# Chunks of 128 tokens computed as two halves of 64 with a state between them, in a fused attention and feed-forward kernel

## The chip, the cores and the metric

The kernel runs on one core of a Trainium2 chip, as one launch. The metric is the time of the device for the whole kernel in microseconds (us), the median of its runs. Five engines work beside each other, each in its own order: TensorE (PE: matmuls into PSUM), VectorE (DVE), ScalarE (ACT), GpSimd (POOL) and SyncE (SP, which starts transfers). They wait for one another through semaphores. All arithmetic is in f32.

## What is computed

Two blocks follow each other. The first is an attention block with a decaying state for each of 4 sequences and 8 heads of 48, over 768 tokens. The second is a feed-forward block over the 3072 rows of 384 that come out.

```python
# batch, n_heads, seq, head_dim = (4, 8, 768, 48)
for t in range(S):
    kt, vt, rt = (k[:, :, t], v[:, :, t], r[:, :, t])
    cur = np.einsum('bhd,bhe->bhde', u[None] * kt, vt)
    y[:, :, t] = np.einsum('bhd,bhde->bhe', rt, state + cur)
    state = w[None, :, :, None] * state + np.einsum('bhd,bhe->bhde', kt, vt)
# x: (3072, 384) from y;  d_ff = 1024
h = x @ w_in
h_max = np.max(h, axis=-1, keepdims=True)
e = np.exp(h - h_max)
sm = e / (np.sum(e, axis=-1, keepdims=True) + 1e-09)
solu = h * sm
mu = np.mean(solu, axis=-1, keepdims=True)
var = np.mean((solu - mu) ** 2, axis=-1, keepdims=True)
ln = (solu - mu) / np.sqrt(var + 1e-06) * g_ln
out = ln @ w_out
```

The recurrence over tokens is computed in chunks. Within a chunk, the tokens meet through a matrix of scores (r and k, each weighed by powers of w, of which only the part with earlier keys counts; the diagonal, with u, is computed apart). What lies before the chunk comes in through the state.

## The kernel before, where the change touches it

There are 24 chunks, called units: 6 chunks in each of 4 sequences, in the order chunk by chunk, sequence by sequence. Unit i is the attention of one chunk; its feed-forward input stage (`ffn_in`, the tensor `h_ps`) comes two units later and its output stage (`ffn_out`, `o_ps`) five further on. The instructions stand in the order in which they are written here; nothing is moved by a scheduler. The file also holds a general path, taken only if the data leave certain ranges; with these inputs it does not run, and no part of what follows is about it.

For one unit, `turn_r` and `turn_k` transpose r and k on TensorE (the first nine units; later ones are transposed by transfers, through the buffers `halves`), `diagonal` writes the own term of every token into AT, `scores` computes keys times queries, `take_scores` copies the part with earlier keys into AT, `heads` adds state times r and v times AT to y, `take_y` copies y out of PSUM, `outer` makes k times v, and `update` moves the state on.

```python
    T, P = 128, 64               # tokens of a chunk, rows of a head (48 used)
    # ... cut ...
    psA = ctx.enter_context(tc.tile_pool(name="psA", bufs=1, space=PSUM))
    psH = ctx.enter_context(tc.tile_pool(name="psH", bufs=1, space=PSUM))
    psM = ctx.enter_context(tc.tile_pool(name="psM", bufs=2, space=PSUM))
    # ... cut ...
    units = [(b, c) for c in range(C) for b in range(B)]
    # ... cut ...
    pss = [psA.tile([128, HP, T], F32, name=f"at{n}") for n in range(4)]
    for ps in pss[:2]:
        nc.vector.memset(ps, 0.0)
    # ... cut ...
    def diagonal(i):
        X = live[i]
        AT = X["AT"] = apool.tile([128, H, T], F32, name="AT", bufs=3)
        for h in range(H):
            nc.scalar.activation(out=AT[:, h, :], in_=ident, func=ACT.Copy, scale=X["own"][:, h])

    def turn_r(i):
        rT = factors(i)["rT"]
        ps = pss[2]
        for a in range(HP):
            nc.tensor.transpose(ps[:, a, :], pair(rpads[i % NLD], a), ident)
        nc.vector.tensor_mul(rT, ps, fore)

    def turn_k(i):
        X = live[i]
        ps = pss[3]

        for a in range(HP):
            nc.tensor.transpose(ps[:, a, :], pair(X["kp"] if i > 0 else kpads[0], a), ident)
        if i > 0:
            nc.scalar.copy(out=X["kT"], in_=ps)
        else:
            nc.vector.tensor_mul(X["kT"], ps, back)

    def scores(i):
        X = live[i]
        ps = pss[2:] if i > LA + LO and i % 2 else pss[:2]
        for a in range(HP):
            for c in range(2):
                for q in range(2):
                    rows = slice(q * P, q * P + D)
                    nc.tensor.matmul(ps[q][ts(c, P), a, c * P :], X["kT"][rows, a, ts(c, P)],
                                     X["rT"][rows, a, c * P :], start=True, stop=True)
        X["scores"] = ps

    def take_scores(i):
        A4 = live[i]["AT"].rearrange("p (a q) t -> p a q t", q=2)
        for q in range(2):
            nc.vector.copy_predicated(A4[:, :, q, :], later.to_broadcast([128, HP, T]),
                                      live[i]["scores"][q])

    def parts(m):

        a, n = divmod(m, 3)
        at = {0: [(0, 0)], 1: [(0, 32), (1, 64)], 2: [(1, 96)]}[n]
        return [(2 * a + q, a * 2 * (D + 32) + off) for q, off in at]

    inner = [[(m,) + p for m in range(g, 12, 4) for p in parts(m)] for g in range(4)]
    inner = [group[n] for n in range(4) for group in inner]

    def heads(i):
        b, c = units[i]
        X = live[i]
        vt, AT, St = vts[i % NV], X["AT"], states[b]
        vf = vt.rearrange("p h d -> p (h d)")
        y_ps = psM.tile([128, KD, 128], F32, tag="m", name="y_ps")
        last = {m: n for n, (m, h, at) in enumerate(inner)}
        opened = set()

        def into(m, lhsT, rhs, stop):
            j, g = divmod(m, 4)
            nc.tensor.matmul(y_ps[32 * g : 32 * g + 32, j, :], lhsT, rhs, start=(g not in opened),
                             stop=stop, skip_group_check=True)
            opened.add(g)

        if c > 0:
            for m in range(12):
                a, n = divmod(m, 3)
                into(m, St[:, a].rearrange("p q d -> p (q d)")[:, ts(n, 32)], X["rT"][:, a, :],
                     False)
        for n, (m, h, at) in enumerate(inner):
            into(m, vf[:, at : at + 32], AT[:, h, :], last[m] == n)
        X["y"] = y_ps

    def take_y(i):
        X = live[i]
        X["xT"] = fpool.tile([128, KD, 128], F32, name="xT", bufs=LA + 1)
        nc.scalar.copy(out=X["xT"], in_=X["y"])

    def outer(chunks):

        chunks = [i for i in chunks if i < N and units[i][1] < C - 1]
        if not chunks:
            return
        kv_ps = psM.tile([128, 2, HP, D], F32, tag="m", name="kv_ps")
        for n, i in enumerate(chunks):
            X, vt = live[i], vts[i % NV]
            X["kv"] = kv_ps[:, n]
            for a in range(HP):
                for g in range(4):
                    h = 2 * a + g // 2
                    nc.tensor.matmul(X["kv"][ts(g, 32), a], X["kp"][:, h, ts(g % 2, 32)],
                                     vt[:, h, 0:D], start=True, stop=True)

    def update(i):
        b, c = units[i]
        if c == C - 1:
            return
        kv_ps, St = live[i]["kv"], states[b]
        for q in range(2):
            wT = pw[ts(q, P), 0, 7].unsqueeze(2).to_broadcast([P, HP, D])
            S = St[ts(q, P), :, q]
            if c > 0:
                nc.vector.tensor_add(S, kv_ps[ts(q, P)], S)
                nc.gpsimd.tensor_mul(S, S, wT)
            else:
                nc.vector.tensor_mul(S, kv_ps[ts(q, P)], wT)
```

The loop over units has an opening, in which one unit is done per turn beside the conversion of the weights (`convert_a` is a ScalarE pass, `low`), and a steady part with two units per turn. The opening, cut to the order of the steps that matter here:

```python
    for i in range(-2, LA + LO):                  # LA, LO = 2, 5
        j = i - LA
        # ... cut: loads ...
        if i >= LA:
            ffn_in(j)
        # ... cut ...
        for p in now:
            convert_a(p)
            # ... cut ...
        if -2 < i:
            turn_r(i + 2)
            if i >= LA:
                unit(j)
            if i < 0 or i >= LA:
                sum_own(i + 2)
            turn_k(i + 2)
        # ... cut ...
        if 0 <= i + 1:
            scores(i + 1)
            take_scores(i + 1)
        # ... cut ...
        if 0 <= i:
            heads(i)
            take_y(i)
            outer([i])
            update(i)
        # ... cut ...
        if 0 <= i:
            diagonal(i + 2)
        # ... cut ...
```

The steady part, with what the change moves:

```python
    for i in range(LA + LO, N + LA + LO, 2):
        # ... cut: loads, decay_k, decay_r, weigh, deviation, halve_ln, diagonal, join_ln, join_rk ...
        if j < N and not late:
            ffn_in(j)
            unit(j)
        # ... cut ...
        ffn_out(l)
        # ... cut ...
        if j + 1 < N:
            ffn_in(j + 1)
        # ... cut ...
        if j + 1 < N:
            unit(j + 1)
        if i == N - 1:
            heads(i)
            take_y(i)
        ffn_out(l + 1)
        # ... cut ...
        now = [n for n in (i + 1, i + 2) if n < N]
        for n in now:
            scores(n)
        for n in now:
            take_scores(n)
        now = [n for n in (i, i + 1) if n < N]
        for n in now if i < N - 1 else []:
            heads(n)
            take_y(n)
        if late:
            halve_rk(i + 4)
        outer(now)
        for n in now:
            update(n)
        # ... cut ...
```

`unit` reads h: ScalarE's exp, VectorE's product with h, then two passes of ScalarE.

## Time and profile before

| what | value |
|---|---|
| time, median of 3 runs | 353.0 us (352.12 to 353.31) |
| span of the profiled execution | 350.7 us |
| granted TensorE clock, mean | 0.998 |
| instructions in the trace | 8480 |
| data moved by transfers | 52.76 MB, mean 150 GB/s |

A profile's page gives, for each engine, how long it was busy and its share of the span; then the span in 40 slices, where each digit is the busy share of a slice in tenths (9 is 90% or more); then the chain of work that ended last, followed back from the last instruction, as shares by engine and by line. Further views list groups of instructions (line, engine, operation, tiles, shapes, count, then busy us and mean ns of one, then idle time of the engine before them and what ended it) and instructions in order of time (start, duration, engine, line, operation, and in brackets idle time before it). "PEld" is TensorE's loading of weights, which overlaps with its matmuls. `128*32 128x64` means 128 rows of contraction, 32 columns of weights, and 64 columns that stream through. Matmuls are pipelined, so their durations overlap; starts say more than durations. The lines on which the reading rests are shown in the prediction.

### The profile page before, as it was taken

Reading aid. Unit: us, or ns where it says so; the run is one execution under the profiler, and the core shown is the slowest. Engines: PE = TensorE matmul, PEld = TensorE weight load, DVE = VectorE, ACT = ScalarE, POOL = GpSimd, SP = SyncE. Lnnn points to the kernel's source line nnn. Section 1 sums busy time; section 2 is a strip of 40 time slices with the busy share of each in tenths; the row PEclk is TensorE's granted clock in tenths of the full one; section 3 lists DMA queues with packets and bytes.
Section 4 is the critical chain, followed back from the end, with each engine's and each line's share of the span. In section 5 each row is a group of like instructions: output and inputs, shape, how many; then the busy total and the mean of one; then the engine's idle time right before and its main releaser. Section 6 shows DMA issues by size and latency. Waiting matters only on the chain.

```text
span 350.7 us, 8480 instructions
## 1 busy us (share of the span) xinstructions
PE 334.1 (95%) x3427; PEld 204.6 (58%) x3427; DVE 210.7 (60%) x347; ACT 240.3 (69%) x457; POOL 179.0 (51%) x196
## 2 busy tenths in 40 slices
PE   2699999999999999999999999999999999999993
PEld 2485566655664665575575575575575475555563
DVE  7795888896477568378368368469466162323420
ACT  3765988988858966866866866866867755546510
POOL 3889667789259449539539529629624000000000
PEclk9999999999999999999999999999999999999999
DMA  7999996269999999887999989855993723554541
GB/s 168 265 241 237 234 209 94 46 104 196 186 179 163 225 188 134 195 151 130 182 157 147 202 146 136 202 127 109 144 172 62 129 68 64 125 127 101 135 104 33
DMA packets 164877, 52.76 MB, mean 150 GB/s; under 512 B 157916, under 2 KB 161244, under 8 KB 164828
## 3 DMA queue, kind: packets, MB, share of 16 engines
q1 hardware_dynamic: 164684, 51.92, 79.6%
q8 instruction: 29, 0.48, 0.6%
q10 hardware_dynamic: 144, 0.20, 0.2%
q14 instruction: 20, 0.16, 0.2%
HBM read 26.94 MB, written 4.72 MB: 90 GB/s over the span
## 4 chain that ended last, share of the span: by engine, by line
PE 81%; ACT 7%; DMA 3%; issue 2%; DVE 2%; POOL 2%; SPq 0%; ACTq 0%; POOLq 0%; DVEq 0%
PE o_ps L896 34%; PE h_ps L814 30%; PE y_ps L761 9%; PE at L728 5%; ACT AT L693 3%; ACT halves L864 2%; DVE solu L826 1%; DMA halves<-halves 1%; PE kv_ps L791 1%; ACT e L817 1%; DMA g_sb<-in_moe_g_ln_dram 1%; POOL kp L669 1%; DMA wq<-in_w_dram 1%; ACT solu L828 1%; ACT e L829 1%
## 5 line engine op out<-in xcount | busy, mean ns | idle before, releaser
L814 PE MATMUL h_ps<-w_in_sb,xT 128*128 128x512 f32 x288 | 129.0, 597 | 1.6 <-DVE ma L534 0.8
L896 PE MATMUL o_ps<-w_out_sb,lnT 128*128 128x384 f32 (+1 forms) x400 | 127.5, 474 | 0.1
L896 PEld LDWEIGHTS o_ps<-w_out_sb,lnT 128*128 128x128 f32 x400 | 74.9, 190 | 53.1 <-issue 8.1
L814 PEld LDWEIGHTS h_ps<-w_in_sb,xT 128*128 128x128 f32 x288 | 53.5, 190 | 63.2 <-issue 57.4
L804 POOL TENSOR_TENSOR state<-state,pw 64x192 f32<-64x192 f32 x32 | 27.6, 861 | 68.8 <-DVE state L803 67.2
L693 ACT ACTIVATE AT<-ident,own 128x128 f32<-128x128 f32 x192 | 58.6, 390 | 5.0 <-DVE own L687 5.0
L864 ACT COPY halves<-solu 128x2048 uint16<-128x2048 uint16 x24 | 45.4, 1892 | 3.1 <-DMA halves<-halves 3.1
L669 POOL TENSOR_TENSOR kp<-kpad,kdec 128x512 f32<-128x512 f32 x24 | 41.6, 1735 | 6.9 <-ACT kdec L623 6.3
L828 ACT ACTIVATE solu<-solu,st 128x1024 f32<-128x1024 f32 x24 | 27.5, 1146 | 24.3 <-DVE solu L826 24.3
L817 ACT ACTIVATE e<-h_ps 128x1024 f32<-128x1024 f32 x24 | 24.4, 1019 | 25.3 <-PE h_ps L814 25.2
L735 DVE COPY_PREDICATED AT<-later,at 128x512 f32<-128x512 uint32 x48 | 31.7, 731 | 15.2 <-PE at L728 15.2
L858 DVE COPY lnT<-halves 128x2048 uint16<-128x2048 uint16 x24 | 33.6, 1420 | 6.9 <-DMA halves<-halves 6.6
L824 DVE RECIPROCAL st<-sums 128x1 f32<-128x1 f32 x24 | 3.9, 163 | 54.4 <-ACT e L817 54.1
L835 POOL TENSOR_SCALAR st<-st 128x1 f32<-128x1 f32 x24 | 7.3, 304 | 49.3 <-ACT e L829 49.2
L826 DVE SCALAR_TENSOR_TENSOR solu<-h_ps,st,e 128x1024 f32<-128x1024 f32 x24 | 30.8, 1284 | 2.1
L858 DVE COPY rk<-halves 128x2048 uint16<-128x2048 uint16 x15 | 29.3, 1956 | 0.0
L777 ACT COPY xT<-y_ps 128x384 f32<-128x384 f32 x24 | 11.5, 478 | 22.4 <-PE y_ps L761 22.4
L683 POOL TENSOR_TENSOR rku<-rku,rpad 128x384 f32<-128x384 f32 x23 | 25.6, 1114 | 1.8
L761 PE MATMUL y_ps<-AT,vt 128*32 128x128 f32 x768 | 26.3, 279 | 0.0
L898 ACT ACTIVATE o<-o_ps,st 128x384 f32<-128x384 f32 (+1 forms) x25 | 13.8, 554 | 18.0 <-PE o_ps L896 11.3
L728 PE MATMUL at<-rk 48*64 48x128 f32 (+1 forms) x768 | 26.2, 266 | 0.0
L829 ACT ACTIVATE e<-solu 128x1024 f32<-128x1024 f32 x24 | 25.4, 1057 | 0.8
(83 smaller groups left out, 345.5 us busy)
## 6 DMA issues: line engine op xcount, KB each, us to landing
raw<-in_moe_w_in_dram SPq DMA_DIRECT2D x12, 512.0 KB, 5.4
raw<-in_moe_w_out_dram SPq DMA_DIRECT2D x16, 384.0 KB, 4.3
kpad<-in_k_dram SPq DMA_DIRECT2D x24, 192.0 KB, 5.1
rpad<-in_r_dram SPq DMA_DIRECT2D x24, 192.0 KB, 5.4
vt<-in_v_dram SPq DMA_DIRECT2D x24, 192.0 KB, 5.0
out_dram<-o SPq DMA_DIRECT2D x23, 192.0 KB, 3.4
halves<-halves SPq DMA_TRANSPOSE x39, 4.9
u_bc<-in_u_dram ACTq DMA_DIRECT2D x1, 192.0 KB, 3.6
```

Source lines behind the costliest of these rows:

```text
L669: nc.gpsimd.tensor_mul(X["kp"].rearrange("p h d -> p (h d)"), kpads[i % NLD].rearrange("p h d -> p (h d)"), kdec.rearrange("p a d -> p (a ...
L693: nc.scalar.activation(out=AT[:, h, :], in_=ident, func=ACT.Copy, scale=X["own"][:, h])
L728: nc.tensor.matmul(ps[q][ts(c, P), a, c * P :], X["kT"][rows, a, ts(c, P)], X["rT"][rows, a, c * P :], start=True, stop=True)
L735: nc.vector.copy_predicated(A4[:, :, q, :], later.to_broadcast([128, HP, T]), live[i]["scores"][q])
L761: nc.tensor.matmul(y_ps[32 * g : 32 * g + 32, j, :], lhsT, rhs, start=(g not in opened), stop=stop, skip_group_check=True)
L814: nc.tensor.matmul(h_ps[:, ts(n, NX)], X["xT"][:, j, :], w_in_sb[:, j, ts(n, NX)], start=(j == 0), stop=(j == KD - 1))
L826: nc.vector.scalar_tensor_tensor(out=solu, in0=X["h"], scalar=rs, in1=X["e"], op0=ALU.mult, op1=ALU.mult, accum_out=tot)
L828: nc.scalar.activation(out=solu, in_=solu, func=ACT.Identity, scale=-float(dff), bias=tot)
L829: nc.scalar.activation(out=X["e"], in_=solu, func=ACT.Square, accum_out=ss)
L858: nc.vector.tensor_copy(out=words.bitcast(U16).rearrange("p n (t o) -> p o n t", o=2), in_=turned)
L864: nc.scalar.copy(out=both.rearrange("p (o n) -> p o n", o=2), in_=split(X["solu"]))
L896: nc.tensor.matmul(o_ps, X["lnT"][:, f, :], w_out_sb[:, f, part], start=(f == 0), stop=(f == KF - 1))
```

## The change

Every chunk of 128 tokens is still one unit, but its attention is computed as two halves of 64 tokens. Scores are only formed between tokens of the same half, so a block of 64 x 64 for each half replaces the 128 x 128 block of which only one triangle counts. What the second half needs of the first comes through a middle state, which is the state before the chunk plus k times v of the first half. The products of v and scores then have 64 tokens on each side: those of the first half lie in the upper 64 rows of TensorE's array, those of the second half in the lower 64 rows, and both can be in the array at once. k times v is split into the two halves in the same way, because the middle state needs the first alone.

PSUM is dealt out anew. Scores take two banks instead of four, with two units side by side in each. y of one half lies in one bank, y of the other in another. In the opening, the transposes of r and k use the two rotating buffers of `psM` that y uses too. In the steady part, y of the first unit of a pair lies in the two banks of `h_ps`.

The diff, cut to its core:

```diff
-    pss = [psA.tile([128, HP, T], F32, name=f"at{n}") for n in range(4)]
-    for ps in pss[:2]:
-        nc.vector.memset(ps, 0.0)
+    pss = [psA.tile([128, 2, HP, U], F32, name=f"at{q}") for q in range(2)]      # U = 64
...
     def diagonal(i):
-        AT = X["AT"] = apool.tile([128, H, T], F32, name="AT", bufs=3)
+        AT = X["AT"] = apool.tile([128, H, U], F32, name="AT", bufs=3)
         for h in range(H):
-            nc.scalar.activation(out=AT[:, h, :], in_=ident, func=ACT.Copy, scale=X["own"][:, h])
+            nc.scalar.activation(out=AT[:, h, :], in_=same, func=ACT.Copy, scale=X["own"][:, h])
...
     def turn_r(i):
-        ps = pss[2]
+        ps = psM.tile([128, HP, T], F32, tag="m", name="tr_ps")
...
     def turn_k(i):
-        ps = pss[3]
+        ps = psM.tile([128, HP, T], F32, tag="m", name="tk_ps")
...
     def scores(i):
         for a in range(HP):
             for c in range(2):
                 for q in range(2):
-                    nc.tensor.matmul(ps[q][ts(c, P), a, c * P :], X["kT"][rows, a, ts(c, P)],
-                                     X["rT"][rows, a, c * P :], start=True, stop=True)
+                    nc.tensor.matmul(pss[q][ts(c, U), i % 2, a, :], X["kT"][rows, a, ts(c, U)],
+                                     X["rT"][rows, a, ts(c, U)], start=True, stop=True)
...
-    def heads(i):
+    def within(i, shared=False):
+        if shared:
+            both = psH.tile([128, dff], F32, tag="h", name="y_ps")
+            y = [both[:, c * NX : c * NX + KD * U] for c in range(2)]
+        else:
+            y = [psM.tile([128, KD * U], F32, tag="m", name="y_ps") for _ in range(2)]
...
+        for n, (m, h, at) in enumerate(inner):
+            j, g = divmod(m, 4)
+            for c in range(2):
+                nc.tensor.matmul(X["y"][c][ts(g, 32), j, :], vf[ts(c, U), at : at + 32],
+                                 AT[ts(c, U), h, :], start=(g not in opened), stop=closes,
+                                 skip_group_check=True)
...
+    def carried(i):
+        for c, St in enumerate((states[units[i][0]], X["mid"])):
+            if c == 0 and units[i][1] == 0:
+                continue
+            for m in range(12):
+                nc.tensor.matmul(X["y"][c][ts(g, 32), j, :],
+                                 St[:, a].rearrange("p q d -> p (q d)")[:, ts(n, 32)],
+                                 X["rT"][:, a, ts(c, U)], start=False, stop=True, ...)
...
     def take_y(i):
-        nc.scalar.copy(out=X["xT"], in_=X["y"])
+        for c in range(2):
+            nc.scalar.copy(out=X["xT"][:, :, ts(c, U)], in_=X["y"][c])
...
     def outer(chunks):
-                    nc.tensor.matmul(X["kv"][ts(g, 32), a], X["kp"][:, h, ts(g % 2, 32)],
-                                     vt[:, h, 0:D], start=True, stop=True)
+                    for c, dst in enumerate(X["kv"]):
+                        nc.tensor.matmul(dst[ts(g, 32), a], X["kp"][ts(c, U), h, ts(g % 2, 32)],
+                                         vt[ts(c, U), h, 0:D], start=True, stop=True)
+
+    def middle(i):
+        for q in range(2):
+            to, kv = X["mid"][ts(q, P), :, q], X["kv"][0][ts(q, P)]
+            if c > 0:
+                nc.vector.tensor_add(to, kv, St[ts(q, P), :, q])
+            else:
+                nc.scalar.copy(out=to, in_=kv)
 
     def update(i):
-            if c > 0:
-                nc.vector.tensor_add(S, kv_ps[ts(q, P)], S)
-                nc.gpsimd.tensor_mul(S, S, wT)
-            else:
-                nc.vector.tensor_mul(S, kv_ps[ts(q, P)], wT)
+            nc.vector.tensor_add(S, X["kv"][1][ts(q, P)], X["mid"][ts(q, P), :, q])
+            nc.gpsimd.tensor_mul(S, S, wT)
...  the opening: outer(i) and middle(i) right after ffn_in(j); turn_k before unit(j)
         if i >= LA:
             ffn_in(j)
+            outer([i])
+            middle(i)
...
             turn_r(i + 2)
+            turn_k(i + 2)
             if i >= LA:
                 unit(j)
-            if i < 0 or i >= LA:
                 sum_own(i + 2)
-            turn_k(i + 2)
...  the steady part
-        now = [n for n in (i + 1, i + 2) if n < N]
+        now = [n for n in (i, i + 1) if n < N - 1] if i < N - 1 else []
+        for n in (i + 1, i + 2):
+            if n < N:
+                scores(n)
+        if now:
+            outer(now)
+        if i + 1 < N:
+            take_scores(i + 1)
         for n in now:
-            scores(n)
+            middle(n)
+        if i + 2 < N:
+            take_scores(i + 2)
         for n in now:
-            take_scores(n)
-        now = [n for n in (i, i + 1) if n < N]
-        for n in now if i < N - 1 else []:
-            heads(n)
+            within(n, n == i)
+        for n in now:
+            carried(n)
             take_y(n)
-        outer(now)
         for n in now:
             update(n)
```

## The prediction

> **What bounds the kernel now.** I read the page first: the busy shares, the forty slices, and the chain that ended last by engine and by line.

> ```profile
> PE 334.1 (95%) x3427; PEld 204.6 (58%) x3427; DVE 210.7 (60%) x347; ACT 240.3 (69%) x457; POOL 179.0 (51%) x196
> PE   2699999999999999999999999999999999999993
> PE 81%; ACT 7%; DMA 3%; issue 2%; DVE 2%; POOL 2%; SPq 0%; ACTq 0%; POOLq 0%; DVEq 0%
> ```

> TensorE is 95% busy and carries 81% of the chain; only the first slices are not full. A busy TensorE need not be a full one, so the second view is TensorE's instructions in order of time, for one pair of chunks in the steady loop.

> ```profile
> 148.06 1.96 PE L728 MATMUL at<-rk 48*64 48x128 f32 x64
> 149.95 0.86 PE L761 MATMUL y_ps<-rk,state 128*32 128x128 f32 x24
> 150.63 1.06 PE L761 MATMUL y_ps<-AT,vt 128*32 128x128 f32 x32
> 151.50 0.84 PE L761 MATMUL y_ps<-rk,state 128*32 128x128 f32 x24
> 152.16 1.06 PE L761 MATMUL y_ps<-AT,vt 128*32 128x128 f32 x32
> 153.03 0.86 PE L791 MATMUL kv_ps<-vt,kp 128*32 128x48 f32 x64
> 153.83 5.42 PE L814 MATMUL h_ps<-w_in_sb,xT 128*128 128x512 f32 x12
> ```

> Read start to start: scores of two chunks 1.89 us, the four y groups 3.08, kv 0.80: the attention stage of a pair takes 5.77 us, the feed-forward stages after it about 20.8, and the pattern returns every 26.6 us. Every f32 matmul leaves two records. The third view is the groups with shapes kept apart.

> ```profile
> L728 PE MATMUL at<-rk 48*64 48x128 f32 x384 | 26.2, 286 | 0.0
> L728 PE MATMUL at<-rk 48*64 48x64 f32 x384 | 21.2, 245 | 0.0
> L761 PE MATMUL y_ps<-AT,vt 128*32 128x128 f32 x768 | 26.3, 279 | 0.0
> L761 PE MATMUL y_ps<-rk,state 128*32 128x128 f32 x480 | 17.1, 275 | 0.0
> L791 PE MATMUL kv_ps<-vt,kp 128*32 128x48 f32 x640 | 9.8, 206 | 0.2 <-issue 0.2
> ```

> A mean of 206 to 286 ns against far shorter starts means records overlap on different tiles of the array. In the single records of the trace one tile takes its next record after 109 ns with 128 columns, 42.5 ns with 48, and about 58 ns with 64 (the scores' second half, where it has work). Records for other tiles start 6.7 ns apart. So two things set a group: columns per tile, and 6.7 ns per record.

> The scores show the waste that the change is after: the upper 64 rows of keys stream 128 columns, 16 records at 109 ns for a pair, 1.74 us of the 1.89, while the tiles of the 64-column half stand idle part of the time.

> [...] 64 kv records take 0.80 us, and their mean pitch is 10.6 ns. [...] the pair loses about 0.29 us over pure streaming at three changes, so about 0.1 us each. [...]

> **The change, part by part, for a steady pair.** Before, pure streaming: scores 16 x 0.109 = 1.74; y per chunk 6 + 8 steps of four tiles at 0.109, for two chunks 3.06; kv 16 x 0.0425 = 0.68; sum 5.48, plus 0.29 for the changes of mode = 5.77.
> - Scores: all blocks 64 x 64, 16 steps of 0.058 = 0.93 (−0.81).
> - V times scores: 32 matmuls per chunk, on eight tiles (two row halves, four column groups), 64 columns. A tile needs 56 ns (scaled between the 42.5 and the 109), eight records need 8 x 6.7 = 53, so 7 ns a record: 128 records 0.91 instead of 1.75 (−0.84).
> - State times r: twice as many, half as wide, still four tiles: 24 steps of 56 ns = 1.34 instead of 1.31. Nothing saved.
> - kv: 128 records on eight tiles, now bound by records: 128 x 6.7 = 0.86 instead of 0.68 (+0.18).
> - One more change of mode (64x64, 64x32, 128x32): +0.1.

> After: 0.93 + 0.86 + 0.91 + 1.34 + 0.39 = 4.43 us. I add 0.1 for a new wait: the first chunk's y now lies in the banks of h, so the next h matmul waits for two ScalarE copies of 192 columns (about 0.22 each from 0.38 for 384, plus some 0.35 of signals), and the second chunk's 0.68 us of state products hides all but this. So 4.53, a saving of 1.25 us per pair.

> Beside TensorE: the predicated copies halve (0.65 to about 0.39 us, four per pair), VectorE gains four adds of 0.38 us for the middle state; that is about +0.5 us on an engine with 17.0 of 26.6 busy. ScalarE's eight diagonal writes fall from 0.306 to about 0.25 each, 0.9 us less per pair. In the attention stage the middle state should be there at 2.8 us, TensorE wants it at 3.05: close, but no wait.

> **The first 80 us are another matter.** Here turning r and k by TensorE used two banks of its own; now it shares the two rotating buffers with y. The second half of y therefore waits until ScalarE has copied kT out. In the changed program that copy stands behind exp and the weight conversion; before it came later still, but y did not wait for it. ScalarE's instructions of the kernel before, in order of time:

> ```profile
> 59.71 1.02 ACT L817 ACTIVATE e<-h_ps 128x1024 f32<-128x1024 f32 x1 [1.05 <-PE h_ps L814]
> ...
> 60.72 1.01 ACT L519 ACTIVATE low<-raw 128x384 uint32<-128x384 uint32 x2
> ...
> 64.62 0.57 ACT L715 COPY rk<-at 128x512 f32<-128x512 f32 x1
> ```

> From the end of h: about 1.1 for exp, 0.93 for the conversion, 0.47 for kT, 0.5 more where the middle state is a ScalarE copy (first chunk of each sequence): kT is out after 2.55 or 3.05 us. TensorE would reach y after 1.93 (0.97 transposes, 0.43 kv, 0.53 scores). With 0.45 and 0.34 to 0.67 of products to follow, the gap between two h stages is 3.8 to 3.95 us, against 3.2 to 3.9 now. So from 36 to 78 us the change brings nothing, or loses a little. The start may come 0.2 us sooner (VectorE and ScalarE do less before it).

> After that, at 98 to 110 us, ScalarE is late behind a transposing transfer; the chain in order of time:

> ```profile
> 98.50 5.07 DMA halves<-halves
> ...
> 103.64 1.90 ACT halves L864
> 105.55 2.35 ACT AT L693 x8
> 107.89 1.01 ACT e L817 x2
> ...
> 110.54 5.42 PE h_ps L814 x12
> ```

> TensorE alone would get there 1.6 us sooner; ScalarE, with three times eight lighter diagonal writes on this way (3 x 0.43), about 1.3 to 1.4. I take 1.4 us at 110.54.

> **Sum.** 1.4 + five pairs x 1.25 = 6.25 + pair 19/20 1.1 (kv half needed where there was none, before 5.43) + pair 21/22 0.75 (before 5.09, now 0.68 of kv that was not there) + last chunk 0.1 = 9.6 us. 353.0 − 9.6 = 343.4 us.

> **Rivals.** (a) Records cost more than 6.7 ns in the new mode, or upper and lower rows do not run at once: for it, no 64x32 tiles in the profile before; against it, the scores' 64x64 tiles. Then V times scores stays at 1.75 and kv goes to 1.36, the pair saves about 0, and the kernel lands near 353, or above it. (b) Waits on ScalarE and VectorE eat the gain, as y, its copies and the middle state are now links in one chain inside a stage shorter by a fifth: for it, the 0.25 us of slack above; against it, ScalarE idle 1.6 us before each xT copy. A wait of 0.5 us per pair makes 347. (c) Transfers become the bound: the share of the 16 DMA engines is 0.87 to 1.04 in the steady stretches. Against it: the stretch at 94 to 121 us ran at 1.13 with TensorE busy 26.72 of 27.0, and the transposes of the loop land several us before their use. Then 350. (d) The first 80 us do better, as pairs of matmuls shrink there too and ScalarE has less to do: 341.

> **Range and chances.** The pair's saving is 1.25 ± 0.4 over eight pairs, ± 3 us, the opening ± 2; together about ± 4, a little longer towards slow: 339 to 349. Faster by over 2% means under 345.9: 0.74; slower by over 2%: 0.03.

> **What would show it.** In the changed profile, a pair's attention stage of about 4.5 us; scores of a pair under 1.1 us; V times scores at about 7 ns a record; kv longer than now by 0.2 us; TensorE waits for ScalarE's kT copy inside y in the first 80 us and no wait for the middle state in the loop; h stages up to 78 us at the times of before. I am wrong if a record of the new groups costs over 10 ns, or if waits of TensorE on ScalarE or VectorE sum to over 5 us after 110 us.

## The result and the profile after

The change makes the kernel slower: 417.56 us (416.61 to 419.48) against 352.92 us for the kernel before on the same chip, a ratio of 1.184 (95% interval 1.180 to 1.189). The prediction was 343.4 us with a range of 339 to 349. One run of the experiments below, 415.11 us of the kernel with one burst, was in the slower state that some executions show.

The page of the changed kernel, its engines, TensorE's busy tenths and granted clock in 40 slices, the queue that the page calls instruction, and the chain that ended last:

```profile
PE 351.5 (85%) x5539; PEld 210.8 (51%) x5539; DVE 212.3 (51%) x385; ACT 236.5 (57%) x491; POOL 181.3 (44%) x206
PE   2778999999599779869949959969978979789994
PEclk9999899999989989989989999998999999969998
q8 instruction: 45, 0.74, 0.7%
PE 11%; ACT 0%; issue 0%
```

TensorE was 95% busy and is now 85% busy. Its slices dip to 4 to 7 in a regular pattern, and so does its clock (0.998 on average before, 0.959 now). The other engines' shares are smaller than before (ScalarE 57% instead of 69%, VectorE 51% instead of 60%, GpSimd 44% instead of 51%), so none of them has become the bound. The chain of the changed kernel breaks off after 11% of the span and is of no use here. The row that turned out to matter is an inconspicuous one, the instruction queue: 45 packets of 16 KB. In the kernel before it reads:

```profile
q8 instruction: 29, 0.48, 0.6%
```

The attention stage of one pair in the steady part, TensorE in order of time (start, duration, line, tile shape, columns, count, idle time before it):

```profile
138.76 1.16 PE L734 MATMUL at<-rk 48*64 48x64 f32 x64
139.85 1.38 PE L807 MATMUL kv_ps<-vt,kp 64*32 64x48 f32 x125
...
143.43 1.46 PE L772 MATMUL y_ps<-AT,vt 64*32 64x64 f32 x122 [2.08 <-issue]
144.81 0.31 PE L785 MATMUL y_ps<-rk,state 128*32 128x64 f32 x5
147.54 0.47 PE L785 MATMUL y_ps<-rk,state 128*32 128x64 f32 x18 [2.42 <-issue]
...
149.47 1.22 PE L839 MATMUL h_ps<-w_in_sb,xT 128*128 128x512 f32 x1
```

The stage took 10.71 us (138.76 to 149.47) where it had taken 5.77. Two gaps of over 2 us lie in it, one a few records into V times scores and one inside a run of like matmuls (state times r). "Issue" says that nothing the profile knows released them: no engine, no transfer of data. The groups with shapes kept apart, at the end of each line idle time and its releaser:

```profile
L772 PE MATMUL y_ps<-AT,vt 64*32 64x64 f32 x1536 | 24.2, 229 | 25.5 <-issue 23.7 <-ACT rk L723 1.6
L807 PE MATMUL kv_ps<-vt,kp 64*32 64x48 f32 x1408 | 17.7, 217 | 3.9 <-issue 3.8
L785 PE MATMUL y_ps<-rk,mid 128*32 128x64 f32 x576 | 16.7, 249 | 8.4 <-issue 8.4
L734 PE MATMUL at<-rk 48*64 48x64 f32 x768 | 16.0, 232 | 0.0
L785 PE MATMUL y_ps<-rk,state 128*32 128x64 f32 x480 | 14.0, 251 | 5.1 <-issue 5.1
```

These issue waits sum to 41 us; in the kernel before they were 0.2 us.

**Where the gaps lie.** Take TensorE's records in order, weight loads, matmuls and its own semaphore and control instructions counted one each, as all are instructions. In the changed kernel all 20 gaps of over 0.7 us that are put down to issue, and one that the view puts down to ScalarE (0.81 us at 117.94), come before a record whose number leaves 193 when divided by 256. The other waits of over 0.7 us, for transfers and engines, do not. The packets of the instruction queue, 16 KB each, follow TensorE's count: 11160 instructions make 44 blocks of 256 and 45 packets are listed, the kernel before has 6927, which make 28 blocks, and 29 packets are listed. So the gaps lie where a new block of 256 begins, by these counts one packet to a block. Single entries of the trace show the order of events; here for the two gaps of the pair above:

```
block entered   last record   next block's first record   packet of the instruction queue
139.88          141.14        143.43                      starts 141.11, takes 0.88
143.43          144.90        147.54                      starts 145.15, takes 0.93
```

From entering one block to executing the first instruction of the next takes 3.5 and 4.1 us, though the 256 instructions were used up after 1.3 and 1.5 us. Over all 21 gaps it is 2.6 to 5.6 us, 4.1 in the mean. The kernel before has one trace of this that I passed over: its single issue wait (0.2 us in the groups shown before, at 126.86 us) also lies at a record with remainder 193. It was already at the edge.

**The clock.** The trace's record of the granted clock lists nine stretches at half speed, seven of 3.413 us and one of twice that within the span, and one at its end. The kernel before has none before its end. In a stage that such a stretch falls into, large matmuls take longer:

```profile
182.41 7.11 PE L839 MATMUL h_ps<-w_in_sb,xT 128*128 128x512 f32 x12
```

The same stage takes 5.42 us at full clock, 1.69 less, about half of the stretch's 3.41. The stretch from 148.43 us follows the two gaps of 2.08 and 2.42 us above, with 1.7 us of matmuls between them. What sets a stretch off is in no view.

### The profile page after: what moved, and what is told of

Its sections match the earlier page's. It is cut to its first block, busy times and chain, and to the rows that moved or that the text cites. A ratio compares the mean times of both kernels' runs of the same rounds, so it can differ in the third digit from the quotient of the medians.

```text
span 414.9 us, 12795 instructions
## 1 busy us (share of the span) xinstructions
PE 351.5 (85%) x5539; PEld 210.8 (51%) x5539; DVE 212.3 (51%) x385; ACT 236.5 (57%) x491; POOL 181.3 (44%) x206
## 5 line engine op out<-in xcount | busy, mean ns | idle before, releaser
L839 PE MATMUL h_ps<-w_in_sb,xT 128*128 128x512 f32 x288 | 135.3, 621 | 0.8 <-ACT xT L794 0.8
L794 ACT COPY xT<-y_ps 128x192 f32<-128x192 f32 x48 | 13.3, 320 | 71.9 <-PE y_ps L785 69.6
L701 ACT ACTIVATE AT<-same,own 128x64 f32<-128x64 f32 x192 | 48.4, 337 | 3.5 <-DVE own L695 3.5
L772 PE MATMUL y_ps<-AT,vt 64*32 64x64 f32 x1536 | 24.2, 229 | 25.5 <-issue 23.7
L677 POOL TENSOR_TENSOR kp<-kpad,kdec 128x512 f32<-128x512 f32 x24 | 35.7, 1491 | 6.4 <-ACT kdec L628 5.8
L883 DVE COPY rk<-halves 128x2048 uint16<-128x2048 uint16 x15 | 32.7, 2178 | 0.0
L772 PEld LDWEIGHTS y_ps<-AT,vt 64*32 64x32 f32 x1536 | 18.9, 107 | 26.4 <-issue 23.4
L690 POOL TENSOR_TENSOR rku<-kpad,u_bc 128x384 f32<-128x384 f32 x23 | 29.8, 1297 | 0.0
L684 POOL TENSOR_TENSOR rp<-rpad,rdec 128x512 f32<-128x512 f32 x15 | 28.2, 1879 | 0.0
L830 DVE TENSOR_TENSOR state<-kv_ps,mid 64x192 f32<-64x192 f32 x40 | 14.1, 354 | 27.2 <-PE y_ps L785 26.6
```

Source lines behind the costliest of these rows:

```text
L677: nc.gpsimd.tensor_mul(X["kp"].rearrange("p h d -> p (h d)"), kpads[i % NLD].rearrange("p h d -> p (h d)"), kdec.rearrange("p a d -> p (a ...
L684: nc.gpsimd.tensor_mul(X["rp"].rearrange("p h d -> p (h d)"), rpads[i % NLD].rearrange("p h d -> p (h d)"), rdec.rearrange("p a d -> p (a ...
L690: engine.tensor_mul(rku, kpads[i % NLD][:, :, 0:D], u_bc)
L701: nc.scalar.activation(out=AT[:, h, :], in_=same, func=ACT.Copy, scale=X["own"][:, h])
L772: nc.tensor.matmul(X["y"][c][ts(g, 32), j, :], vf[ts(c, U), at : at + 32], AT[ts(c, U), h, :], start=(g not in opened), stop=closes, skip_ ...
L839: nc.tensor.matmul(h_ps[:, ts(n, NX)], X["xT"][:, j, :], w_in_sb[:, j, ts(n, NX)], start=(j == 0), stop=(j == KD - 1))
```

## The experiments

**Theory.** TensorE runs out of instructions. Each matmul of the program leaves two records, each with a weight load (the 32 matmuls of a pair's scores leave 64 records; the page lists 5539 matmul records and 5539 weight loads): four instructions. The pair's attention stage had 240 records, 480 instructions, in 5.8 us; now it has 416 records, 832 instructions, in one burst of tiny matmuls. **Rival.** The new tiles (64 rows by 32 columns, upper and lower rows) or the middle state stall by themselves in a way that the profile doesn't show. My texts for the runs count instructions where they say records: the "830 TensorE records" of the first are the 832 instructions, and the "384" and "128 more records" of two later ones are 192 and 64 records.

### The same matmuls, standing apart

The opening is that of the kernel before (units 0 to 6 in chunks of 128). In the steady part the scheme of the change is kept, but its pieces stand between the feed-forward stages:

```diff
     ffn_in(j)
+    outer_two(mine)                  # k times v of both chunks
     ffn_out(l)
+    within(i, "y"); carried(i)       # V times scores, state times r
     ffn_in(j + 1)
+    scores(i + 1); scores(i + 2)
     ffn_out(l + 1)
-    scores, outer, within, carried of both chunks in one burst
+    within(i + 1, "y"); carried(i + 1)
```

> Opening as in the kernel before; from then on the split scheme of the change with the same matmuls and tile shapes, but its pieces stand apart, each between two feed-forward stages (at most some 300 TensorE records between two stages of large matmuls, where the change has some 830 in a row). Theory (TensorE runs out of instructions: they arrive in blocks of 256, some 4 us each, and the changed attention stage asks for more than three blocks at once): the 1 to 4 us gaps that no engine explains go away, and so do the stretches at half clock; 350 to 356 us. Rival (the tiles of 64 x 32 in upper and lower rows stall by themselves, or wait for the middle state): the gaps stay with the pieces; 395 us or more.

Measured: 356.63 us (356.57 to 357.21), ratio to the kernel before 1.010 (1.008 to 1.013), clock 0.997. TensorE in order of time:

```profile
153.51 0.86 PE L855 MATMUL at<-AT,vt 64*32 64x64 f32 x64
154.29 0.54 PE L865 MATMUL at<-rk,state 128*32 128x64 f32 x24
154.65 0.52 PE L865 MATMUL at<-rk,mid 128*32 128x64 f32 x24
155.10 5.42 PE L921 MATMUL h_ps<-w_in_sb,xT 128*128 128x512 f32 x12
160.45 1.43 PE L886 MATMUL at<-vt,kp 64*32 64x48 f32 x128
161.81 5.43 PE L1003 MATMUL o_ps<-w_out_sb,lnT 128*128 128x384 f32 x16
167.16 0.86 PE L855 MATMUL at<-AT,vt 64*32 64x64 f32 x64
```

This is just above the range of the supply theory (350 to 356), and far from the rival's 395. No issue wait is left on any of these groups. The tiles are the same and the matmuls are the same in number, so the rival falls, but for the banks of PSUM, which are dealt out differently here; the repeated k times v below, in the banks of before, leaves no room for that. The largest piece is now 128 records, 256 instructions, and it comes after 5.35 us in which TensorE used a few dozen.

### The change in one burst, with the opening of before

As the last kernel, but the pieces of a pair together, as the change has them:

```diff
-    ffn_in(j); outer_two(mine); ffn_out(l); within(i, "y"); carried(i)
-    ffn_in(j + 1); scores(i + 1); scores(i + 2); ffn_out(l + 1); ...
+    ffn_in(j); ffn_out(l); ffn_in(j + 1); ffn_out(l + 1)
+    scores(i + 1); scores(i + 2); outer_two(now); within, carried of i and i + 1
```

> Opening as in the kernel before, then the split scheme in one burst per pair of chunks, as the change has it. Both theories: some 12 us less than the changed kernel, as its h stages in the first 85 us start 12 us later than before: about 405 us, with the gaps in the steady part as they were. If the opening's loss does not add up with the rest, 400 or 417.

Measured: 405.03 us (401.83 to 415.11), 1.147 (1.138 to 1.155); the median without the run of 415.11 us is 402.75 us. Its issue waits, from the view of waits (sum, times, longest):

```profile
PE y_ps L855 <- issue: 17.0, 8, 3.7
PE y_ps L865 <- issue: 11.8, 6, 2.5
PE at L886 <- issue: 5.6, 3, 2.2
```

This splits the whole loss. 417.56 − 405.03 = 12.5 us come from the changed opening (14.8 with the median of three); 405.03 − 356.63 = 48.4 us (46.1) from having the pieces in one burst; 356.63 − 353.2 = 3.4 us from the split itself with its pieces apart, where the change was to save some 8 us.

### The kernel before with more records of k times v

Nothing of the change is in these two. The matmuls k times v of the steady part are issued twice or four times over, each time into the same place:

```diff
-            for a in range(HP):
+            for _ in range(2 if len(chunks) == 2 else 1):      # or 4
+              for a in range(HP):
                 for g in range(4):
                     nc.tensor.matmul(X["kv"][ts(g, 32), a], ...)
```

> The kernel before with nothing of the change in it; only the matmuls k times v of the steady part are issued four times over into the same place: 384 more records per pair of chunks, all of 128 rows, 2.04 us of array time per pair, eight pairs. Theory of the instruction supply: 860 records in a burst run dry, gaps of 1 to 4 us every 256 instructions with no engine behind them and stretches at half clock; 390 us (378 to 405). Rival (the split tiles are at fault, not the count): 353 + 8 x 2.04 = 369 us, no such gaps.

> As the fourfold one, but k times v twice: 128 more records per pair, 0.68 us of array time per pair. Theory of the instruction supply: 363 us (358 to 368), as the burst of 600 records just overruns the supply. Rival: 353 + 8 x 0.68 = 358 us with no gaps.

Measured: fourfold 398.31 us (394.80 to 399.88), 1.124 (1.119 to 1.130), clock 0.972; twofold 365.06 us (363.59 to 366.41), 1.035 (1.030 to 1.039), clock 0.996. The fourfold kernel's run of k times v in one pair:

```profile
133.90 1.35 PE L792 MATMUL kv_ps<-vt,kp 128*32 128x48 f32 x106
138.06 1.57 PE L792 MATMUL kv_ps<-vt,kp 128*32 128x48 f32 x128 [2.81 <-issue]
142.61 0.46 PE L792 MATMUL kv_ps<-vt,kp 128*32 128x48 f32 x22 [2.98 <-issue]
```

The issue waits of the twofold kernel (sum, times, longest):

```profile
PE kv_ps L792 <- issue: 4.8, 4, 2.8
PE h_ps L815 <- issue: 2.6, 1, 2.6
```

Both times are those of the supply theory (390 and 363), not those of the rival (369 and 358). The expectations counted eight pairs; only six have two chunks that need k times v, as the trace's 6 x 384 = 2304 more instructions show, so that the rival comes to 365 and 357 and is further off still. In the fourfold kernel 128 records stand between the two gaps shown, the 256 instructions of one block. The ten gaps over 0.7 us in the fourfold kernel all lie at remainder 193 again, and so do the five issue waits of the twofold (three over 0.7 us, two of 0.64 and 0.29). The sum for the twofold: 6 x 0.68 = 4.1 us of array time and 7.4 us of issue waits make 11.5, of the 11.9 measured, with no stretch at half clock before its end. For the fourfold, 6 x 2.04 = 12.2 us and 25.4 us of issue waits make 37.6, of the 45.1 measured; its trace lists 20.5 us at half clock before the end, which by an estimate cost at most half of that, 10.2 us. Full-height tiles of 32 columns, without upper and lower rows or a middle state, stalled in the same way here (2.81 and 2.98 us in the pair shown) once they were enough in number.

### Do upper and lower rows run at once?

```diff
-            for n, (m, h, at) in enumerate(inner):
-                for c in range(2):
+            for c in range(2):
+                for n, (m, h, at) in enumerate(inner):
```

> The kernel whose pieces stand apart, with one thing changed: in V times scores the twelve-plus-four matmuls of the upper rows all come before those of the lower rows, so only one half of the rows is in use at a time. If upper and lower rows do run at once when they alternate, V times scores costs more here: 14 ns a record (half of the 27 ns of a 128-column record in the kernel before) instead of the 12 measured with alternation, 64 records x 2 ns x 17 units = 2 us more, and more still if the alternating order had a floor of its own. If they don't, the order is without effect: within 0.5 us of the same.

Measured: 357.58 us (357.35 to 359.00), 1.013 (1.009 to 1.016); beside 1.010 (1.008 to 1.013) the intervals overlap, so the total does not decide. The stage does:

```profile
166.56 0.99 PE L855 MATMUL at<-AT,vt 64*32 64x64 f32 x64
167.49 0.54 PE L865 MATMUL at<-rk,state 128*32 128x64 f32 x24
```

V times scores takes 0.93 us from start to start, where the alternating order took 0.78 or 0.79. That is 0.14 x 17 = 2.4 us of TensorE's time; some of it replaced waits (the 0.8 us for the middle state are gone). The starts of single records tell more. Nanoseconds from one record to the next, alternating order, the first 32 records and some after them:

```
7 6 7 7 6 7 7 33 7 6 7 7 6 7 7 9 6 7 7 6 7 7 6 10 6 7 7 6 7 7 6 29
55 9 16 17 17 16 11 6 11 6 11 5 11 6 11 6 ...
```

The second and the third eight records take 56 ns each, where the prediction gave one tile alone 56 ns for one record: the two row halves do run at once, and 7 ns a record is right, for 32 records. Then the pace falls to two records in 17 ns, or one in 17. k times v shows the same after about as many (in the changed kernel from 36.48 us, 32 records in 0.20 us, later two in 17 ns).

### Mixing the pieces

This was to find a version that beats both kernels. In each piece, records that take 14 ns stand between groups of 32 that take 7 ns:

```diff
-    within(i, "y"); carried(i)
+    weave(within(i, "y"), carried(i), [(16, 12), (16, 12)])        # matmuls
-    outer_two((i, i + 1)); ...; scores(i + 1); scores(i + 2)
+    weave(outer_two(i), scores_two(i), [(16, 16), (16, 0)])         # one chunk per piece
```

The finer mix alternates 4 matmuls with 3, and 4 with 2.

> The kernel whose pieces stand apart has four pieces per pair of chunks: k times v of both, scores of both, and V times scores with state times r once for each. Its records show 7 ns for the first 32 matmuls of a piece and 8.4 ns or more for the rest, with a pause of 0.1 us where it changes. Here each piece is mixed: 32 records of k times v, 32 of the scores, 32 of k times v; and 32 of V times scores, 24 of state times r, 32, 24. If the 7 ns come from 32 records that stand ready in a queue, which is refilled while slower records (14 ns) run, a pair loses about 0.35 us in V times scores and 0.3 us in k times v: 27.04 to about 26.4 us, 351 us (349 to 354). If it is something else (the tiles or the addresses of the second half of the records), the time stays at 356 to 357.5.

> The same pieces mixed finely: 8 records of V times scores, 6 of state times r, and so on; 8 of k times v, 4 of scores, and so on. If changes between tile shapes cost nothing, it gains another 0.2 us a pair over the coarse mix: 349 us. If each of the some 60 changes a pair costs 20 to 30 ns, a pair is 1.2 to 1.8 us longer: 361 to 366 us.

Measured: coarse 359.75 us (359.40 to 360.16), 1.020 (1.018 to 1.021); fine 429.29 us (427.30 to 431.41), 1.218 (1.214 to 1.221). Both miss what I expected. The coarse mix:

```profile
153.59 0.45 PE L860 MATMUL at<-AT,vt 64*32 64x64 f32 x32
153.97 0.54 PE L872 MATMUL at<-rk,state 128*32 128x64 f32 x24
154.44 0.46 PE L860 MATMUL at<-AT,vt 64*32 64x64 f32 x32
154.83 0.54 PE L872 MATMUL at<-rk,mid 128*32 128x64 f32 x24
155.30 5.42 PE L951 MATMUL h_ps<-w_in_sb,xT 128*128 128x512 f32 x12
```

The first half of the expectation holds: single records show all 64 records of V times scores at 7 to 8 ns (238 ns from the first to the last of each 32), so it is not the addresses of the second half, and a stock of about 32 records that refills during slower ones fits, though no view shows one. What I had left out is the change of shape: the last record before another shape holds TensorE for 132 to 149 ns instead of the 9 to 36 ns between groups of the same shape. The trace has 58 more such changes than that of the kernel whose pieces stand apart; 58 x 0.146 = 8.5 us outweigh the gain, 8 x 0.65 = 5.2 us by the expectation, and the 3.3 us between them agree with the 3.1 measured. The fine mix shows it bare:

```profile
158.53 0.31 PE L872 MATMUL at<-rk,state 128*32 128x64 f32 x6
158.77 0.32 PE L860 MATMUL at<-AT,vt 64*32 64x64 f32 x8
159.01 0.31 PE L872 MATMUL at<-rk,state 128*32 128x64 f32 x6
```

A group of 8 or of 6 records takes 0.24 us, where 8 records at 7 ns are 0.06. With 392 more changes (23 per chunk) it loses 72.7 us to the kernel whose pieces stand apart: 0.19 us each, of which the last record before a change accounts for 0.15. My "20 to 30 ns" was at least five times too little. It has no gap at a block boundary.

### Two pieces per pair

```diff
     ffn_in(j)
-    outer_two(mine)
+    outer_two(mine); scores(i); scores(i + 1)                       # 384 instructions
...
     ffn_out(l + 1)
-    within(i + 1, "y"); carried(i + 1)
+    within(i), within(i + 1), carried(i), carried(i + 1)            # 448 instructions
```

> The kernel whose pieces stand apart, with four pieces per pair put together to two: k times v and scores of both chunks after one feed-forward stage (192 records, so 384 instructions with their weight loads), V times scores and state times r of both after another (224 records, 448 instructions). Fewer changes of tile shape (6 for 10 a pair) would save 0.5 us a pair. Rival to the instruction supply (only the number of shape changes and of pieces counts): 356.6 - 8 x 0.5 = 352.5 us. Theory of the supply (256 instructions per block, about 3.9 us from entering a block to having the next): a piece of 384 crosses two block boundaries in half of the cases, one of 448 in three of four, each time some 2.3 us of waiting: 8 x (1.2 + 1.7) = 23 us more, 376 us (365 to 388), with gaps at block boundaries again.

Measured: 373.37 us (370.45 to 374.27), 1.056 (1.050 to 1.062), clock 0.981. The theory of the supply had 376, the count of shape changes 352.5. In the piece of 448:

```profile
163.84 0.48 PE L865 MATMUL at<-rk,state 128*32 128x64 f32 x19 [1.60 <-issue]
```

Six gaps over 0.7 us, at remainder 193, with 3.1 to 5.1 us from entering a block to entering the next. There were fewer of them than I had reckoned, and other waits had appeared (3.3 us of scores on VectorE), so the close hit is partly luck. It shows the trend: largest piece 256 instructions, no gap; 384 and 448, some; 832, two or three in every pair. The rate counts too: the kernel before has 480 in one stage, spread over 5.8 us, and only its 0.2 us of waiting.

No version of the split came below the kernel before. With the largest piece at 256 instructions it needs four pieces, and their shape changes cost more than the split saves (356.63 us against 353.2); with two pieces it runs out of instructions (373.37), with one as well (405.03).

## Why the prediction was wrong

**What bounds the kernel before.** "TensorE is 95% busy" and its pair of 26.6 us were read rightly. What was missed is that TensorE can wait for instructions, as it then did for 41 us in the changed kernel. The 480 instructions in 5.8 us passed with next to none: the one issue wait of 0.2 us, which stood in a line I quoted, was the sign.

**The sum for a pair failed at its basis, that only array time and 6.7 ns per record set a group.** It held no limit on how many instructions can follow each other. The text counted the records (416 for 240) and did not ask what brings them. This one omission costs about 48.4 us of 64.4 in the steady part. Issue waits are 34.4 us in the kernel with one burst. The rest has two parts: one wait of 3.8 us for ScalarE at the last chunk, and the half clock, at which its trace lists 30.7 us between the opening and the end. If these cost half their length, 15.4 us at most, the three exceed the 48.4 by 5.2, and some 0.7 us a pair that the pieces standing apart pay on their side (below) are about as much. This is an estimate; no run separates the half clock from the gaps. They go together over the runs. Between the opening and the end, the traces list 27.3 us at half clock in the changed kernel (30.7 with the stretch in its opening), 30.7 in the one with one burst, 20.5 in the fourfold, 10.2 in the one with two pieces per pair, and none in the twofold and in the kernels without gaps, but for the fine mix: it has 10.2 us without a gap, so the gaps are not the only thing that it came with.

**The terms of the sum, measured where no instruction is missing** (the kernel whose pieces stand apart, start to start, with the shape changes in them):

| per pair, us | predicted | measured |
|---|---|---|
| scores | 0.93 | 1.10 |
| k times v | 0.86 | 1.36 |
| V times scores | 0.91 | 1.56 |
| state times r | 1.34 | 1.62 |
| changes of mode, new wait | 0.49 | in the lines above |
| pair, with feed-forward | 25.35 | 27.04 |

- Scores and state times r are right: without the 0.14 us at their end they take 0.96 and 1.34.
- **"7 ns a record" is right for 32 records only.** Less the changes, k times v is 1.22 (+0.36) and V times scores 1.28 (+0.37). I had taken 6.7 ns from groups whose columns left time between fast groups of three or four records (in k times v of the kernel before 6, 7 and 7 ns, then 22), and carried it over to a row of 128.
- A change of mode is 0.13 to 0.15 us at the end of a group, not 0.1. The "0.35 of signals" for the new wait is near what the kernel before shows: its copy of y starts 0.34 us after the last record of y (153.28 after 152.94). Feed-forward stages next to small pieces take 5.35 us from start to start instead of 5.16 to 5.25. Two more changes (2 x 0.14) and three more such stages (3 x 0.15) make about 0.7 us per pair that the change, in one burst, would not have.

Even with instructions at hand the change would have gained next to nothing, by an estimate that no run tests: 27.04 less 0.7 is 26.3 us a pair, where 26.6 was to be beaten. The stage shown above took 10.71 us, less 4.50 of waits that is 6.2 us, 1.04 of them at half clock; 5.77 was to be beaten. So rival (a), "records cost more than 6.7 ns ... the pair saves about 0 ... 353", named the right term; of its two reasons the first is right, and the second is not, as the rows do run at once.

**Rival (b) came true in one place, (c) not at all.** After 110 us TensorE waits 4.6 us in all for ScalarE, in two places; for VectorE not at all. One of the two, 0.8 us, lies at a block boundary. The other, 3.8 us before 364.31 us, comes at the last chunk, for which the sum had a gain of 0.1 us: the output stage waits for ScalarE's two copies of y, which start at 363.96, behind the last two passes of another chunk's `unit`:

```profile
364.31 8.38 PE L921 MATMUL o_ps<-w_out_sb,lnT 128*128 128x384 f32 x16 [3.83 <-ACT xT L794]
```

The middle state was in time, as predicted. The DMA share fell, to 0.65 and 0.71 in the two pairs from 149.50 to 216.00 us, against 0.87 before.

**The first 80 us.** The waits for ScalarE's kT copy came where they were predicted:

```profile
39.95 0.69 PE L772 MATMUL y_ps<-AT,vt 64*32 64x64 f32 x44 [0.79 <-ACT rk L723]
41.53 0.41 PE L772 MATMUL y_ps<-AT,vt 64*32 64x64 f32 x18 [0.88 <-issue]
...
42.34 7.11 PE L839 MATMUL h_ps<-w_in_sb,xT 128*128 128x512 f32 x12
...
52.89 0.84 PE L772 MATMUL y_ps<-AT,vt 64*32 64x64 f32 x62 [0.83 <-ACT rk L723]
```

But the h stages, "3.8 to 3.95 us" apart by the prediction, stand 4.3 us or more apart even without a wait (from 59.48, the end of one, to 63.78), and the stage at 84.65 starts where 72.69 was its place: 12 us late, as the 12.5 us between the two openings have it. Of these, 4.8 us are issue waits (2.7 of them in one, before the first h stage) and 1.7 a stage at half clock. Full clock also came later at the start: the trace's list of the clock opens at full speed at 28.96 us, in the kernel before at 21.98, and until then matmuls are slow (a turn of r takes 1.12 us at 25.48 us, before 0.66 at 22.40). What brought it later, and the rest of the 12 us, no run shows. "Rival (d): 341" had the wrong sign.

**The conditions for being wrong** were the right ones in part: records of k times v and V times scores did cost 9.5 to 12 ns. None looked at waits that no engine releases, and these were the largest.

## What to carry to other kernels

Count TensorE's instructions per stretch, here four for each f32 matmul, and set them against their supply: here a block of 256 could be used about 4 us after the one before it had been entered, so some 256 tiny matmul instructions between large matmuls passed free, and 832 in a row lost 3 to 6 us. When matmuls are split into smaller tiles, price three things beside the columns: the supply of instructions, the pace, which here was 7 ns per record for only some 32 records and 8.5 ns or more after them, and the changes of tile shape, which here cost some 0.15 us each. A wait named "issue", however small (here 0.2 us), is the sign to look for before splitting further. The packets of the instruction queue alone don't tell, as they only follow the count of instructions: the kernel whose pieces stand apart has 40 and no such wait, the kernel before 29.
